# Moving two half products and chunk 4's turns ahead of the work that needs w_out's third quarter

## The chip, the cores and the metric

The kernel runs on one NeuronCore of a Trainium2 chip. The metric is the device time of one execution in microseconds (us). The program has five instruction streams: TensorE (PE in the profile, with its weight loads as PEld), VectorE (DVE), ScalarE (ACT), GpSimd (POOL) and SyncE (SP). Each works through its own stream in the order in which it was written and waits for the others by semaphores. SP issues nearly all transfers; POOL issues the four that bring w_out, because they change the type from float32 to bfloat16 on the way. Sixteen DMA engines carry both.

## The reference

A recurrent attention layer with one decay per head is followed by a feed-forward layer with a squared ReLU. Batch 4, 8 heads, 768 tokens, head size 64; 3072 tokens of width 512; d_ff is 2048.

```
for t in range(S):
    state = gamma[None, :, None, None] * state + einsum('bhd,bhe->bhde', k[:, :, t], v[:, :, t])
    y[:, :, t] = scale * einsum('bhd,bhde->bhe', q[:, :, t], state)
x = y.transpose(0, 2, 1, 3).reshape(B * S, H * D)
h = maximum(x @ w_in, 0.0)
out = h * h @ w_out
```

## The kernel before

**Tiling.** The 3072 tokens are 24 chunks of 128 tokens, six to a batch. The attention is done chunk by chunk: q and k are scaled by powers of the decay and turned (transposed) so that the head dimension lies on the partitions, the scores of a chunk are formed and masked, the running state is updated, and the outputs become the columns of `xt`, the input of the feed-forward part. The feed-forward part works on blocks of chunks: `BLOCKS` makes the first block four chunks wide and the other ten two chunks wide. A block's first product is `x @ w_in` with ReLU (line 826 for the matmuls, 835 for the ReLU on ACT, 806 for the square on DVE); its second product is `h @ w_out`.

**Seven products for eight.** The second product is in part done as a 2 by 2 block product with seven half-width products instead of eight, on sums of blocks. For the weights these sums are the four tiles `w_sum` (t1 to t4), each made in two halves by `sum_w_out` (line 319): the low half of each needs the first two quarters of w_out, the high half the last two. For the first block, chunks 0 and 1 are multiplied in the plain way and chunks 2 and 3 by seven products. That is `second_products` in `last_of_first`. A call `plain(j)` multiplies two of the sixteen row blocks of w_out for chunks 0 and 1 (four matmuls with 512 columns, line 1017) and adds one matmul with 256 columns to the product pa (line 984). `plain(0)` to `plain(3)` use w_out's first two quarters, `plain(4)` and `plain(5)` the third quarter, `plain(6)` and `plain(7)` the fourth. The products pd (s1 by t1), pb (s2 by t2) and pe (a22 by t4) each have eight matmuls with 256 columns; their low halves (four matmuls, `lo`) need only the low halves of t1, t2 and t4.

**What sets the order.** The order is written out by hand. The feed-forward pieces are generators, and each `yield` ends a piece. After piece n the loop at the end calls `before(n)`, which emits whatever `put(n, ...)` has listed for that place. So PE's order is the pieces with the steps of the next chunks' attention between them, and every other engine gets its part of a step at the same point of its own stream. For chunk m, `attend(m, scaled, places)` lists q's turn at `places[0]` (line 391, copied out of PSUM by ACT at line 397), k's turn at `places[1]` (line 404, copied by ACT at line 411), the scores of the first four heads at `places[2]` and of the other four at `places[3]` (line 430, masked by DVE at line 437), the state also at `places[3]` (line 458, copied by ACT at 481 and DVE at 483), and the outputs at `places[4]` (lines 498 and 506, copied by ACT at 514). Both turns use the one PSUM buffer `tp`, so k's turn waits until ACT has copied q's. The two halves of the scores share the one PSUM buffer `st`.

**The places around the change.** Twelve pieces of the first product end at place 16. In `second_products` the pieces `plain(0)` to `plain(5)` end at places 17 to 22; pd's and pb's low halves at 23; pe's low half at 24; `plain(6)` at 25 and `plain(7)` at 26, where ACT copies pa away (line 1038) and the two plain results (line 1041); pa's remaining eight matmuls, which add to the pa just copied, at 27; pd's high half at 28, pb's at 29, pe's at 30. The w_out sums' low halves are listed at place 20; DVE's sums for s3 and s4 (`last_sums`, line 980) at 22.

**Later chunks.** From chunk 8 on, k is scaled and cast on POOL (line 688) and turned by a transposing transfer that SP issues (line 711, tile `kT`), and the scores are at line 727. SP works through loads, stores and these transfers in one order.

Of the kernel before, what the change touches and what calls it, by code (L numbers as in the profile page):

```python
# [31 lines left out]
def kernel(  # L32
# [280 lines left out]
    def sum_w_out(half):  # L313

        src = w_out_halves[half].rearrange("s (j k) (n c) -> s k n j c", k=2, n=2)
        (b11, b12), (b21, b22) = ([src[:, k, n] for n in range(2)] for k in range(2))
        t1, t2, t3, t4 = (t[:, 4 * half : 4 * half + 4] for t in sums)
        for out, in0, in1 in ((t1, b12, b11), (t2, b22, t1), (t3, b22, b12), (t4, b21, t2)):
            yield nc.vector.tensor_tensor(out=out, in0=in0, in1=in1, op=ALU.subtract)
# [498 lines left out]
    def h_of(tb, f0, f1=None):  # L818
        n = NFB // len(h2s[tb])
        j, f = divmod(f0, n)  # L820
        return h2s[tb][j][:, f : f + (1 if f1 is None else f1 - f0)]
# [137 lines left out]
    def last_of_first():  # L959

        def halves_of(k, c):
            return [
                t.rearrange("e (j k) (c t) -> e k c j t", k=2, c=4)[:, k, 2 + c] for t in h2s[0]
            ]

        (a11, a12), (a21, a22) = ([halves_of(k, c) for k in range(2)] for c in range(2))
        n = NFB // 4
        s1, s2, s4 = (
            [
                t.rearrange("e (x j t) -> e x j t", x=2, t=C)[:, x]  # L970
                for x in range(2)
            ]
            for t in (spare[:, i * HN * 4 : (i + 1) * HN * 4] for i in range(3))
        )
        s3 = a21
        b = lambda k, c: lambda j: w_out_bf[j // 2][:, 2 * (j % 2) + k, c * HN : (c + 1) * HN]
        t1, t2, t3, t4 = (lambda j, t=t: t[:, j] for t in sums)

        def add(out, in0, in1, op=ALU.add):
            nc.vector.tensor_tensor(out=out, in0=in0, in1=in1, op=op)  # L980

        def product(to, left, right, js, start=True, stop=True):
            for j in js:
                nc.tensor.matmul(  # L984
                    to,
                    lhsT=left[j // n][:, j % n],
                    rhs=right(j),
                    start=(start and j == 0),
                    stop=(stop and j == NFB // 2 - 1),
                    skip_group_check=True,  # L990
                )

        def first_sums(x):
            add(s1[x], a21[x], a22[x])
            add(s2[x], s1[x], a11[x], ALU.subtract)

        def last_sums():
            for x in range(2):
                add(s3[x], a11[x], a21[x], ALU.subtract)
            for x in range(2):  # L1000
                add(s4[x], a12[x], s2[x], ALU.subtract)

        def second_products():
            ops = [ps_f.tile([P, DM], FP32, name="psf") for _ in range(2)]
            pa, pe, pd, pb = (
                t[:, n * HN : (n + 1) * HN]
                for t in [ps_f.tile([P, DM], FP32, name="psf") for _ in range(2)]
                for n in range(2)
            )
            oa, ob = (opool.tile([P, DM], FP32, name="osb") for _ in range(2))  # L1010
            a, u, v = (upool.tile([P, HN], FP32, name=f"u{i}") for i in range(3))
            r0 = 2 * C

            def plain(j):
                for f in (2 * j, 2 * j + 1):
                    for c, op in enumerate(ops):
                        nc.tensor.matmul(  # L1017
                            op[:],
                            lhsT=h_of(0, f)[:, 0, c * C : (c + 1) * C],
                            rhs=w_out_bf[f // FPQ][:, f % FPQ, :],  # L1020
                            start=(f == 0),
                            stop=(f == NFB - 1),
                        )
                product(pa, a11, b(0, 0), (j,))

            lo, hi = range(0, 4), range(4, 8)
            for j in range(6):
                plain(j)
                yield
            product(pd, s1, t1, lo)  # L1030
            product(pb, s2, t2, lo, False)
            yield
            product(pe, a22, t4, lo, False)
            yield
            plain(6)
            yield
            plain(7)
            nc.scalar.activation(a[:], pa, AF.Copy)
            for c, op in enumerate(ops):
                osb = opool.tile([P, DM], FP32, name="osb")  # L1040
                nc.scalar.activation(osb[:], op[:], AF.Copy)
                nc.sync.dma_start(out[c * C : (c + 1) * C], osb[:])
            yield
            product(pa, a12, b(1, 0), lo, False)
            product(pa, a12, b(1, 0), hi, False)
            nc.scalar.activation(oa[:, 0:HN], pa, AF.Copy)
            yield
            product(pd, s1, t1, hi)
            yield
            product(pb, s2, t2, hi)  # L1050
            add(u[:], pb, a[:])
            yield
            product(pe, a22, t4, hi)
            yield
            product(pb, s3, t3, lo, False)
            yield
            product(pb, s3, t3, hi, False)
            add(v[:], pb, a[:])
            add(ob[:, HN:DM], pd, v[:])
            add(ob[:, 0:HN], pe, v[:])  # L1060

            def last_product():
                product(pd, s4, b(1, 1), range(8), False)
                add(oa[:, HN:DM], pd, u[:])
                yield
                nc.sync.dma_start(out[r0 + C : r0 + 2 * C], ob[:])
                yield
                nc.sync.dma_start(out[r0 : r0 + C], oa[:])
                yield

            kept.append(last_product())
            yield

        return first_sums, last_sums, second_products
# [174 lines left out]
    def put(place, what, *args):  # L1249
        parts.setdefault(place, []).append((what, args))  # L1250
# [4 lines left out]
    def attend(m, scaled, places):  # L1255
        if m % 2 == 0:
            put(scaled, scale_q, m, 0)
            put(scaled + 2 if m == 4 else scaled, scale_q, m, 1)
            put(places[0], transpose_q, m)
        put(18 if m == 4 else places[0], scale_kv, m)  # L1260
        put(places[1], transpose_k, m)
        put(places[2], scores, m, 0)
        put(places[3], scores, m, 1)
        put(places[3], state, m)
        put(places[4], outputs, m)
# [20 lines left out]
    for m, which, place in ((6, "k", 16), (6, "v", 17), (7, "k", 18), (7, "v", 19)):  # L1286
        put(place, load_kv, m, which)
    put(10, cast_w, "in", 3)
    for half, at_places in enumerate(((20, 20, 20, 20), (23, 23, 27, 27))):
        made = sum_w_out(half)  # L1290
        for place in at_places:
            put(place, next, made)
    attend(4, 13, (21, 22, 24, 26, 29))
    attend(5, None, (25, 28, 30, 32, 34))
    attend(6, 31, (33, 35, 37, 39, 42))
    attend(7, None, (38, 42, 44, 46, 49))
# [74 lines left out]
```

## Time and profile before

| what | value |
|---|---|
| median of three runs | 205.26 us (205.23 to 205.27) |
| the profiled execution's own time | 205.27 us |
| its span, first to last instruction | 203.4 us |
| PE busy | 195.3 us (96% of the span) |
| DVE, ACT, POOL busy | 155.2, 127.2, 66.4 us |
| share of the DMA engines' time, SP's queue and POOL's queue | 72.4% and 6.3% |

The span is what the trace covers; 1.87 us of the execution's time lie around it. PE is the engine that is nearly always busy, so time is to be found where PE stands still or where its work can shrink. A gap of another engine costs nothing unless PE waits for what comes behind it. In the views quoted below a row gives the start in us, a length in us, the engine, the line of the kernel, the operation with its tiles, and how many instructions were merged. Brackets give the idle time of the engine before the row and who ended it. A matmul's length includes its drain, which overlaps the next one, so the time that a matmul holds PE is read from start to start.

### The profile page before, as it was taken

To read this page: it belongs to the slowest core of one execution; us is meant where nothing else is said; L and a number is where in the kernel's file an instruction comes from. 1 tells how busy PE (TensorE), PEld (TensorE's weight loads), DVE (VectorE), ACT (ScalarE), POOL (GpSimd) and SP (SyncE) were. 2 spreads that over 40 slices of the span, in tenths; PEclk is the share of its full clock that TensorE was granted. 3 is DMA by queue.
4 is the path that set the end of the run, shared out by engine and by line. 5 is a ranking of instruction groups with operands and counts; after the bars stand their busy time and mean duration, and the time that the engine had idled before them with its cause. 6 is when DMAs were issued, how large, how long until landed. Compare 5 with 4: busy or idle time off the path is not lost.

```text
span 203.4 us, 5804 instructions
## 1 busy us (share of the span) xinstructions
PE 195.3 (96%) x2346; PEld 162.2 (80%) x2351; DVE 155.2 (76%) x322; ACT 127.2 (63%) x258; POOL 66.4 (33%) x131
## 2 busy tenths in 40 slices
PE   5899998999999999999999999999999999999993
PEld 1478444678975998988989899999989999999883
DVE  3986789768797678788698798798798798485374
ACT  8764871455753776792694784783785775763730
POOL 8693710131300451372234335352225225100000
PEclk9999999999999999999999999999999999999999
DMA  5999999999779596989986997899979642200202
GB/s 174 357 374 398 327 190 196 258 232 297 199 197 229 141 158 126 220 216 226 161 228 122 242 215 171 198 228 187 218 168 204 164 103 58 103 3 0 106 0 103
DMA packets 92250, 38.12 MB, mean 187 GB/s; under 512 B 68544, under 2 KB 88256, under 8 KB 92224
## 3 DMA queue, kind: packets, MB, share of 16 engines
q1 hardware_dynamic: 90112, 35.66, 72.4%
q0 software_dynamic: 2112, 2.10, 6.3%
q8 instruction: 18, 0.29, 0.7%
q14 instruction: 8, 0.07, 0.1%
HBM read 27.26 MB, written 6.29 MB: 165 GB/s over the span
## 4 chain that ended last, share of the span: by engine, by line
PE 73%; DMA 11%; SPq 6%; DVE 4%; ACT 3%; issue 1%; POOL 0%; DVEq 0%
PE psf L826 32%; PE psf L860 18%; PE tp L860 7%; DMA w_out_bf<-in_moe_w_out_dram 6%; DMA stage<-in_moe_w_in_dram 5%; PE psf L1149 3%; SPq L164 3%; SPq L115 2%; PE psf L984 2%; PE y L783 2%; PE st L727 2%; PE y L776 2%; PE c_ps L754 2%; PE psf L1017 1%; DVE h L806 1%
## 5 line engine op out<-in xcount | busy, mean ns | idle before, releaser
L826 PE MATMUL psf<-xt,w_in_bf 128*128 128x256 bf16 (+2 forms) x879 | 92.2, 259 | 0.3 <-issue 0.2
L826 PEld LDWEIGHTS <-w_in_bf 128*128 128x128 bf16 x880 | 71.2, 98 | 11.4 <-issue 0.2
L835 ACT ACTIVATE h<-psf 128x512 bf16<-128x512 f32 x96 | 56.1, 595 | 21.7 <-PE psf L826 20.2
L806 DVE TENSOR_TENSOR h<-h 128x512 bf16<-128x512 bf16 x80 | 35.6, 460 | 18.1 <-ACT h L835 17.9
L688 POOL CAST ks_bdp<-stage 64x512 bf16<-64x512 f32 x32 | 23.0, 718 | 37.6 <-issue 23.3
L705 POOL COPY v_bd<-v 64x512 bf16<-64x512 bf16 x32 | 20.6, 644 | 44.8 <-DVE v L697 35.3
L860 PEld LDWEIGHTS <-h 128*128 128x128 bf16 x288 | 26.3, 98 | 3.6 <-DVE h L806 0.7
L860 PE MATMUL tp<-w_out_bf,h 128*128 128x256 bf16 x136 | 19.4, 273 | 0.2 <-DVE h L806 0.2
L860 PE MATMUL psf<-w_sum,h 128*128 128x256 bf16 x136 | 19.1, 273 | 0.0
L860 PE MATMUL psf<-w_sum,k_bd 128*128 128x256 bf16 x144 | 17.9, 273 | 0.0
L361 DVE TENSOR_TENSOR qs<-qn,qf 128x512 bf16<-128x512 f32 x20 | 16.0, 804 | 0.1
L860 PEld LDWEIGHTS <-k_bd 128*128 128x128 bf16 x144 | 13.7, 98 | 1.5
L856 DVE TENSOR_TENSOR osb<-psf,u 128x256 f32<-128x256 f32 x26 | 10.3, 421 | 6.1 <-PE psf L860 5.8
L763 ACT ACTIVATE s_bd<-c_ps 64x256 bf16<-64x256 f32 x29 | 10.7, 370 | 6.3 <-PE c_ps L754 6.3
L856 DVE TENSOR_TENSOR u<-psf,u 128x256 f32<-128x256 f32 x18 | 7.6, 423 | 8.9 <-PE psf L860 8.8
L697 DVE TENSOR_TENSOR v<-stage,kf 128x512 bf16<-128x512 f32 x16 | 12.5, 780 | 0.0
L764 ACT ACTIVATE s_bd<-c_ps 64x256 bf16<-64x256 f32 x29 | 11.0, 379 | 0.4
L734 DVE TENSOR_TENSOR pt<-st,cmask 128x512 bf16<-128x512 f32 x16 | 11.0, 687 | 0.3 <-issue 0.2
L856 DVE TENSOR_TENSOR k_bd<-h 128x512 bf16<-128x512 bf16 x18 | 10.7, 596 | 0.3
L790 ACT ACTIVATE xt<-y 128x512 bf16<-128x512 f32 x16 | 9.6, 598 | 1.8 <-PE y L783 1.2
L896 ACT ACTIVATE osb<-tp 128x256 f32<-128x256 f32 x8 | 3.1, 384 | 12.2 <-PE tp L860 12.2
L804 ACT ACTIVATE h<-h 128x512 bf16<-128x512 bf16 x16 | 10.1, 630 | 0.5
(145 smaller groups left out, 281.6 us busy)
## 6 DMA issues: line engine op xcount, KB each, us to landing
qn<-in_q_dram SPq DMA_DIRECT2D x12, 512.0 KB, 5.1
out_dram<-osb SPq DMA_DIRECT2D x23, 256.0 KB, 3.0
stage<-in_k_dram SPq DMA_DIRECT2D x32, 96.0 KB, 3.8
stage<-in_v_dram SPq DMA_DIRECT2D x32, 96.0 KB, 3.2
stage<-in_moe_w_in_dram SPq DMA_DIRECT2D x4, 512.0 KB, 7.1
stage<-in_moe_w_in_dram SPq DMA_DIRECT2D x2, 1024.0 KB, 10.2
w_out_bf<-in_moe_w_out_dram POOLq DMA_DIRECT2D x4, 512.0 KB, 10.4
kn<-in_k_dram SPq DMA_DIRECT2D x6, 256.0 KB, 5.9
```

What stands on the lines that cost most here:

```text
L361: engine.tensor_tensor(out=out, in0=by, in1=table[:, :, None].to_broadcast([P, H, D]), op=ALU.mult)
L688: nc.gpsimd.tensor_copy(ks[rows, :, hh, :].rearrange("s (u p) d -> s u p d", u=2), kn[rows])
L697: nc.vector.tensor_tensor(out=v2.rearrange("s (u p) d -> s u p d", u=2), in0=vn, in1=kf2[:, i, :, :, None].to_broadcast([P, 2, NPAIR, D]), ...
L705: nc.gpsimd.tensor_copy(v_bd[rows, :, hh, :], v2[rows])
L734: nc.vector.tensor_tensor(out=pt[:], in0=st[:], in1=cmask2.rearrange("s r t -> s (r t)")[:, None, :].to_broadcast([P, 2 * NPAIR, C // 2]), ...
L763: nc.scalar.activation(s_bd[halves[0], :, 0, :], c[halves[0]], AF.Copy)
L764: nc.scalar.activation(s_bd[halves[1], :, 1, :], c[halves[1]], AF.Copy)
L806: nc.vector.tensor_mul(hv, hv, hv)
L826: nc.tensor.matmul(hp, lhsT=w_in_bf[g][:, cb, fq * 128 : (fq + 1) * 128], rhs=xts[tb][:, cb, cols], start=(cb == 0), stop=(cb == NCB - 1),)
L835: nc.scalar.activation(hv, hp[:], AF.Relu)
L856: nc.vector.tensor_tensor(out=out, in0=in0, in1=in1, op=op)
L860: nc.tensor.matmul(to, lhsT=left[:, j], rhs=right(j) if callable(right) else right[:, j], start=(start and j == 0), stop=(stop and j == NF ...
```

## The change

Three orders change; no instruction is added or taken away. In `second_products` the low halves of pd and pb go ahead of `plain(4)` and `plain(5)`, the first pieces that use w_out's third quarter. The places then end at 20 for `plain(3)`, 21 for the two low halves, 22 and 23 for `plain(4)` and `plain(5)`; from 24 on they are as before. Chunk 4's q is turned at 19 instead of 21, its k at 21 instead of 22, its scores and masks come at 23 and 25 instead of 24 and 26, its state at 25 instead of 26; its outputs stay at 29. The high halves of t1 and t2 go from place 23 to 24, those of t3 and t4 from 27 to 26. On DVE this puts chunk 4's first mask ahead of the high halves of t1 and t2, and its second mask and state copy ahead of chunk 5's k scaling.

```diff
@@ -1024,12 +1024,15 @@
                 product(pa, a11, b(0, 0), (j,))
 
             lo, hi = range(0, 4), range(4, 8)
-            for j in range(6):
+            for j in range(4):
                 plain(j)
                 yield
             product(pd, s1, t1, lo)
             product(pb, s2, t2, lo, False)
             yield
+            for j in range(4, 6):
+                plain(j)
+                yield
             product(pe, a22, t4, lo, False)
             yield
             plain(6)
@@ -1286,11 +1289,11 @@
     for m, which, place in ((6, "k", 16), (6, "v", 17), (7, "k", 18), (7, "v", 19)):
         put(place, load_kv, m, which)
     put(10, cast_w, "in", 3)
-    for half, at_places in enumerate(((20, 20, 20, 20), (23, 23, 27, 27))):
+    for half, at_places in enumerate(((20, 20, 20, 20), (24, 24, 26, 26))):
         made = sum_w_out(half)
         for place in at_places:
             put(place, next, made)
-    attend(4, 13, (21, 22, 24, 26, 29))
+    attend(4, 13, (19, 21, 23, 25, 29))
     attend(5, None, (25, 28, 30, 32, 34))
     attend(6, 31, (33, 35, 37, 39, 42))
     attend(7, None, (38, 42, 44, 46, 49))
```

## The prediction

> **What bounds the kernel now.** I read the page first (busy shares and the chain that ended last), then PE's waits between 24 and 60 us, then the order of instructions around them.
>
> ```profile
> PE 195.3 (96%) x2346; PEld 162.2 (80%) x2351; DVE 155.2 (76%) x322; ACT 127.2 (63%) x258; POOL 66.4 (33%) x131
> PEclk9999999999999999999999999999999999999999
> PE 73%; DMA 11%; SPq 6%; DVE 4%; ACT 3%; issue 1%; POOL 0%; DVEq 0%
> PE psf L1017 <- DMA w_out_bf<-in_moe_w_out_dram: 0.9, 1, 0.9
> PE psf L984 <- DVE w_sum L319: 0.2, 1, 0.2
> ```
>
> PE is the bound, at full granted clock. What can be won by reordering is only the time in which PE stands still, and the two waits say where: in the first block's second product, once for w_out's third quarter, once for a sum of w_out. The order of instructions shows more small gaps beside these two.
>
> ```profile
> 33.84 1.03 PE L1017 MATMUL psf<-w_out_bf,h 128*128 128x512 bf16 x4
> 35.86 1.02 PE L1017 MATMUL psf<-w_out_bf,h 128*128 128x512 bf16 x4 [0.88 <-DMA w_out_bf<-in_moe_w_out_dram]
> 36.83 0.61 PE L391 MATMUL tp<-ident,qs 128*128 128x128 bf16 x8
> 37.27 1.03 PE L1017 MATMUL psf<-w_out_bf,h 128*128 128x512 bf16 x4
> 37.47 1.02 ACT L397 ACTIVATE qT<-tp 128x1024 bf16<-128x1024 bf16 x1 [5.75 <-PE tp L391]
> 38.55 0.38 PE L404 MATMUL tp<-ident,ks 128*128 128x128 bf16 x4
> 38.77 1.47 PE L984 MATMUL psf<-w_sum,h 128*128 128x256 bf16 x12
> 38.97 1.21 ACT L411 ACTIVATE k_bd<-tp 64x512 bf16<-64x512 bf16 x2 [0.47 <-PE tp L404]
> 39.27 0.69 DVE L319 TENSOR_TENSOR w_sum<-w_out_bf 128x1024 bf16<-128x1024 bf16 x1 [1.29 <-DMA w_out_bf<-in_moe_w_out_dram]
> 40.08 0.49 PE L430 MATMUL st<-qT,k_bd 128*128 128x128 bf16 x4
> 40.41 1.03 PE L1017 MATMUL psf<-w_out_bf,h 128*128 128x512 bf16 x3
> 41.38 1.03 PE L1017 MATMUL psf<-w_out_bf,h 128*128 128x512 bf16 x4
> 42.35 0.39 PE L430 MATMUL st<-qT,k_bd 128*128 128x128 bf16 x4
> 42.55 0.38 ACT L1038 ACTIVATE u<-psf 128x256 f32<-128x256 f32 x1 [2.38 <-PE psf L984]
> 42.58 0.39 PE L458 MATMUL c_ps<-v_bd,ks 128*128 128x128 bf16 x4
> 42.78 0.69 DVE L437 TENSOR_TENSOR pt<-st,cmask 128x512 bf16<-128x512 f32 x1 [0.88 <-PE st L430]
> 42.99 1.03 PE L984 MATMUL psf<-w_out_bf,h 128*128 128x256 bf16 x8
> 44.96 0.22 PE L498 MATMUL y<-qT,s_bd 128*128 128x128 bf16 x1
> 45.25 0.68 DVE L319 TENSOR_TENSOR w_sum<-w_out_bf,w_sum 128x1024 bf16<-128x1024 bf16 x1
> 45.99 0.61 PE L984 MATMUL psf<-w_sum,h 128*128 128x256 bf16 x4 [0.20 <-DVE w_sum L319]
> 47.83 1.06 PE L826 MATMUL psf<-xt,w_in_bf 128*128 128x128 bf16 x16
> ```
>
> Start to start, a `plain` piece holds PE 0.97 us (35.86 to 36.83, 40.41 to 41.38), eight turns 0.44 (36.83 to 37.27), four turns, four scores or four state matmuls 0.22 to 0.23 (38.55 to 38.77, 42.35 to 42.58), and twelve half-width matmuls 1.31 (38.77 to 40.08), so 0.109 each: four take 0.44, eight 0.87. Chunk 4's outputs are twelve matmuls of 128 columns, 0.67 at the turns' pace. With these the gaps come out: before `plain(4)` 33.84 + 0.97 = 34.81 to 35.86, **1.05**; before k's turn 37.27 + 0.97 = 38.24 to 38.55, **0.31** (one `tp`: ACT frees it at 38.49); in the first scores 0.33 less 0.23, **0.10** (ACT's copy of k ends at 40.18); before pa's remaining matmuls 42.58 + 0.22 = 42.80 to 42.99, **0.19** (ACT must copy pa first); before pe's high half 44.96 + 0.67 = 45.63 to 45.99, **0.36** (the high half of t4 on DVE ends at 45.93).
>
> **The change part by part.** PE does the same work; I walk it from 33.84, where chunk 4's q turn now stands.
>
> ```profile
> 31.13 0.60 ACT L835 ACTIVATE h<-psf 128x512 bf16<-128x512 f32 x1 [0.27 <-PE psf L826]
> 30.37 0.68 DVE L361 TENSOR_TENSOR qs<-qn,qf 128x512 bf16<-128x512 f32 x1
> 34.34 0.69 DVE L319 TENSOR_TENSOR w_sum<-w_out_bf,w_sum 128x1024 bf16<-128x1024 bf16 x1
> 35.55 1.10 DVE L319 TENSOR_TENSOR w_sum<-w_out_bf,w_sum 128x1024 bf16<-128x1024 bf16 x1
> 37.24 0.74 DVE L980 TENSOR_TENSOR h<-h,h 128x512 bf16<-128x512 bf16 x2
> 44.20 0.43 DVE L483 CAST s_bd<-c_ps 64x256 bf16<-64x256 f32 x1 [0.73 <-ACT s_bd L481]
> ```
>
> *q's turn and `plain(3)`.* q was scaled by 31.05 (30.37 + 0.68), and ACT has nothing between 31.73 and 37.47. Turn 33.84 to 34.28, `plain(3)` to 35.25. ACT copies 0.64 after the turn's start (36.83 to 37.47): 34.48 to 35.50. *The two half products ahead* need the low halves of t1 and t2, ready at 35.03 (34.34 + 0.69): 35.25 to 36.12, no wait. *k's turn* finds `tp` free since 35.50: to 36.34, so the 0.31 goes; ACT copies k 0.42 later (38.55 to 38.97), 36.54 to 37.75. *`plain(4)`* starts at 36.34 where the quarter was usable at 35.86: the 1.05 goes, with 0.48 to spare. `plain(5)` ends at 38.28. *First scores:* k's copy has been done for half a microsecond, so the 0.10 goes; to 38.50. pe's low half (t4 done at 36.65) to 38.94.
>
> *What is late next, the fourth quarter.* DVE could use it at 39.27, after standing idle for it. Before, PE came to `plain(6)` at 40.41 and this arrival was hidden; now it comes at 38.94. I take 39.27 for PE too: a new wait of **0.33**. `plain(6)` to 40.24, scores and state to 40.68.
>
> *`plain(7)` and pa.* From `plain(7)`'s start to pa's remaining matmuls before was 42.99 - 41.38 = 1.61, of which 0.97 is the piece; the rest is ACT's copy (42.55 to 42.93) with the handovers. Before, scores and state lay in it and PE lost 0.19; now they have gone ahead, nothing covers it, and PE waits 0.64, **0.45** more. ACT's state copy goes ahead of the pa copy, but its state is done 0.97 earlier. pa starts at 40.68 + 1.61 = 42.29.
>
> *t4 in time.* DVE now does, in order: first mask (0.43 after the scores' start, as 42.35 to 42.78: 38.71 to 39.40, behind the sums of line 980 that end at 37.98), high t1, high t2, second mask, state copy, chunk 5's k scaling, high t3, high t4. Six of about 0.69 and one 0.43 with no overlap end at 39.40 + 4.57 = 43.97. Should one run 1.10, as the row at 35.55 did, it is 44.38. pe's high half comes at 42.29 + 0.87 + 0.44 + 0.22 + 0.44 + 0.67 = 44.93: the 0.36 goes with half a microsecond to spare at the worst. Queued behind the new wait on DVE are the second mask and chunk 5's scaling, wanted only by its k turn at 43.60. That turn's copy on ACT (0.42 later, 44.02 to 45.23) must be done by the scores at 45.37: 0.14 to spare, which is tight.
>
> *SP and POOL* keep their order; before 44 us no transfer on them waits for what is moved, so I leave the landings where they are.
>
> From pa's remaining matmuls to the next block's first product the old way took 47.83 - 42.99 = 4.84, less 0.36 is 4.48: **42.29 + 4.48 = 46.77, a gain of 1.06 us.** By the gaps: 1.05 + 0.31 + 0.10 + 0.36 - 0.33 - 0.45 = 1.04, the same but for rounding. The profiled execution took 205.27 us (median of the runs 205.26), so 204.2. If the new waits cost nothing the gain would be 1.82, but the 0.45 is a turnaround that the trace shows in full; only the 0.33 is open, from zero (204.2 - 0.33 = 203.9) to the late landing below.
>
> The Trainium skill, "TensorE: Matmul & The Clock Gate", section "Back-to-back issue gap", gives about 131 ns per 512-column and 81 ns per 128-column matmul in a sustained stream. By it, as an estimate with this kernel's rows for the half-width ones, PE would stand before `plain(6)` at 38.33 instead of 38.94, the fourth quarter would cost 0.61 more, and the time would be 204.8. The trace disagrees: a piece of four 512-column matmuls and one of 256 takes 0.97, of which the four are 0.86, or 215 ns each.
>
> **The rivals.**
>
> ```profile
> L170 POOL DMA_DIRECT2D w_out_bf<-in_moe_w_out_dram x4: 742/767/940, 21.9 to 25.3; - x4
> ...
> DMA to landing us min/median/max: 7.1/10.4/13.9
> ...
> kn<-in_k_dram SPq DMA_DIRECT2D x1, 256.0 KB, 15.7
> 78.37 1.27 SPq L711 DMA_TRANSPOSE kT<-ks_bdp  x1
> kT<-ks_bdp SPq DMA_TRANSPOSE x1, 3.3
> kT<-ks_bdp SPq DMA_TRANSPOSE x1, 4.2
> 82.32 0.40 PE L727 MATMUL st<-qT,kT 128*128 128x64 bf16 x8
> ```
>
> *A: transfers that don't move take some back.* PE is 1.06 us early for every later load. The nearest later case is chunk 10's turned k: issued by SP at 78.37, landed 3.3 later at 81.67, used at 82.32. If SP's order doesn't come earlier with PE, PE arrives at 81.26 and waits 0.41: 204.6. For it: SP is busy without a break through these stretches. Against it: part of SP's order waits for stores that PE and ACT release.
>
> *B: no gain is left.* The same transfer at the 4.2 us that chunk 11's took would land at 82.57, later than PE came before: 205.3 or a little over. It needs SP unmoved and a slower landing, both; I give it little.
>
> *C, the slower end: w_out's fourth quarter lands late.* The longest landing of the four w_out transfers, 13.9 us, is this quarter's, from its issue at 25.3 to 39.2. Behind it now stand PE's `plain(6)` and DVE's second mask with nothing to cover them, so each microsecond counts in full. The gain is gone when it lands 1.06 later, at 40.3; at the 15.7 us that chunk 5's k load took in the same stretch it lands at 41.0, 1.73 later than the 39.27: 204.2 + 1.7 = 205.9. Against it: what SP and POOL issue before that is unchanged. The Trainium skill, "DMA: Bandwidth & Descriptors", section "Queues, rings and completion order", says that each DMA engine takes turns between its queues packet by packet; by that, more packets on SP's queue would delay w_out. No row here shows those turns one by one.
>
> **How the numbers follow.** The walk as told 0.67, with 203.9 to 204.4 as its own range; the fourth quarter costing nothing 0.05 (203.9); A 0.13 (204.6); B 0.07; C 0.08. The forecast is the walk's 204.2. The range, 203.8 to 204.9, takes the first three cases, 0.85. About 0.2% (0.4 us) is what can be told from no change: faster 0.85, same 0.07, slower 0.08.
>
> **What would show it.** In the changed profile the wait for w_out's third quarter is gone from PE's list and a wait of about 0.3 us for the fourth stands in front of `plain(6)`; the turn of k follows the half products without a gap; a gap of some 0.6 us stands between `plain(7)` and the next half-width matmuls; no wait for `w_sum` is left; the next block's first product starts near 46.8; chunk 10's scores start near 81.3 without a wait. The prediction is wrong if either quarter's landing moves by more than half a microsecond, or if the gain at 46.8 is not there at the end.

## The result and the profile after

| | before | changed |
|---|---|---|
| median of 18 executions each | 205.29 us (205.16 to 206.04) | 204.52 us (204.05 to 205.28) |
| mean of the same | 205.50 us | 204.59 us |
| ratio of the times | | 0.9956, 95% interval 0.9943 to 0.9968 |
| the profiled execution's own time, span | 205.27, 203.4 us | 204.98, 203.1 us |

The changed kernel is faster by 0.44%: 0.9 us by the ratio and by the means, 0.77 by the medians, 1.11 between the quickest executions. The forecast was 204.2. Both kernels' times here can be split at their widest gap into two groups: 204.05 to 204.57 (eleven) and 204.79 to 205.28 (seven) for the changed one, 205.16 to 205.30 (ten) and 205.53 to 206.04 (eight) for the one before.

The page of the changed kernel, engine shares and chain, and PE's waits between 24 and 60 us:

```profile
PE 195.3 (96%) x2351; PEld 162.2 (80%) x2351; DVE 154.7 (76%) x322; ACT 127.5 (63%) x258; POOL 67.5 (33%) x131
PE 88%; DVE 4%; DMA 3%; ACT 2%; SPq 1%; issue 1%; DVEq 0%
PE psf L984 <- ACT u L1041: 0.5, 1, 0.5
```

PE is as busy as before. The two waits of this stretch, for w_out's third quarter and for a sum of w_out, are gone; a wait of pa's remaining matmuls for ACT is new (the changed file's line 1041 is the pa copy, 1038 before). The chain has 3% of transfers where it had 11%.

PE's order in the changed kernel, from chunk 4's q turn to the next block's first product (rows left out are marked by dots):

```profile
34.61 0.61 PE L391 MATMUL tp<-ident,qs 128*128 128x128 bf16 x8
...
39.92 1.02 PE L1017 MATMUL psf<-w_out_bf,h 128*128 128x512 bf16 x4
...
45.58 0.60 PE L984 MATMUL psf<-w_sum,h 128*128 128x256 bf16 x4
46.02 0.39 PE L430 MATMUL st<-qT,k_bd 128*128 128x128 bf16 x4
...
47.41 0.78 PE L826 MATMUL psf<-xt,w_in_bf 128*128 128x128 bf16 x11
```

From q's turn the stretch takes 47.41 - 34.61 = 12.80 us; before, from the same PE time, it took 47.83 - 33.84 = 13.99. That is 1.19 won. But q's turn itself stands 0.77 later in this execution (34.61 against 33.84), so the next block's product is only 0.42 earlier, and 0.14 is lost further on: 0.28, the difference of the two spans to rounding. The 0.77 doesn't come from the diff. Most of it arose in the program's first 10 us, ahead of everything that the diff moves, as the first scaling on GpSimd shows (changed kernel, then the kernel before):

```profile
8.25 1.23 POOL L559 TENSOR_TENSOR ks_bdp<-kn,kfp 128x512 bf16<-128x512 f32 x1 [2.12 <-DMA kn<-in_k_dram]
```

```profile
7.60 1.26 POOL L559 TENSOR_TENSOR ks_bdp<-kn,kfp 128x512 bf16<-128x512 f32 x1 [1.46 <-DMA kn<-in_k_dram]
```

The first k arrived 0.65 later here; in the later run of the changed kernel (experiment 12) this scaling started at 7.71. So two questions were left for the experiments: are the steps right where the start is the same as in the profile of before, and what does a late start do to either kernel?

### The profile page after: what moved, and what is told of

Its sections match the earlier page's. It is cut to its first block, busy times and chain, and to the rows that moved or that the text cites. A ratio compares the mean times of both kernels' runs of the same rounds, so it can differ in the third digit from the quotient of the medians.

```text
span 203.1 us, 5810 instructions
## 1 busy us (share of the span) xinstructions
PE 195.3 (96%) x2351; PEld 162.2 (80%) x2351; DVE 154.7 (76%) x322; ACT 127.5 (63%) x258; POOL 67.5 (33%) x131
## 4 chain that ended last, share of the span: by engine, by line
PE 88%; DVE 4%; DMA 3%; ACT 2%; SPq 1%; issue 1%; DVEq 0%
PE psf L826 40%; PE psf L860 18%; PE tp L860 7%; PE psf L1017 3%; PE psf L1152 3%; DMA kn<-in_k_dram 3%; PE psf L984 3%; PE y L783 2%; PE st L727 2%; PE y L776 2%; PE c_ps L754 2%; DVE h L806 1%; PE c_ps L627 1%; PE y L506 1%; PE st L430 1%
## 5 line engine op out<-in xcount | busy, mean ns | idle before, releaser
L896 ACT ACTIVATE osb<-tp 128x256 f32<-128x256 f32 x8 | 3.1, 384 | 12.2 <-PE tp L860 12.2
```

## The experiments

**1 and 2: each part alone.** The first keeps the half products' move and puts chunk 4's places and the sums back; the second keeps the places and leaves the products where they were.

```diff
 e1: the changed kernel with
-    for half, at_places in enumerate(((20, 20, 20, 20), (24, 24, 26, 26))):
+    for half, at_places in enumerate(((20, 20, 20, 20), (23, 23, 27, 27))):
-    attend(4, 13, (19, 21, 23, 25, 29))
+    attend(4, 13, (21, 22, 24, 26, 29))
 e2: the changed kernel with
-            for j in range(4):
+            for j in range(6):
                 plain(j)
                 yield
             product(pd, s1, t1, lo)
             product(pb, s2, t2, lo, False)
             yield
-            for j in range(4, 6):
-                plain(j)
-                yield
```

> The half products of pd and pb go ahead of plain(4) and plain(5); chunk 4's places and the w_out sums stay as before. Theory (the gain is PE's wait for the third quarter, everything else only moves from one gap to another): the 1.05 us in front of plain(4) goes, the gaps at k's turn (0.31), at t4 (0.36) and at pa (0.19) stay, no wait for the fourth quarter appears since PE comes to it at about 40.3; the stretch from plain(3)'s start to the next block's first product, 13.99 us before, shrinks by 1.1, as much as in the whole change (predicted 1.06, 1.19 in its profile). Rival (the places carry a good part): it shrinks by 0.7 or less. Time 204.2 against 205.27 by the theory, 204.6 or more by the rival.

> Chunk 4's places and the places of the w_out sums as in the change; the half products stay behind plain(5). Theory: q's turn now stands in front of plain(3), so 0.44 us of the wait for the third quarter is covered and 0.61 is left; the gaps at k's turn (0.31), first scores (0.10) and t4 (0.36) go; pa's wait grows from 0.19 to 0.64; no wait for the fourth quarter, which PE reaches at 39.6. The stretch shrinks by 0.77: time 204.5. Rival (the places only move waits about): the stretch shrinks by 0.4 or less, what q's turn covers.

Measured: the products alone 204.28 us (204.10 to 205.37), ratio 0.9964 (0.9948 to 0.998); the places alone 204.90 us (204.46 to 205.06), ratio 0.9975 (0.9967 to 0.9984). PE's order with the products alone:

```profile
30.92 0.81 PE L1017 MATMUL psf<-w_out_bf,h 128*128 128x512 bf16 x3
...
36.13 1.03 PE L1017 MATMUL psf<-w_out_bf,h 128*128 128x512 bf16 x4
...
37.41 0.38 PE L404 MATMUL tp<-ident,ks 128*128 128x128 bf16 x4
...
44.85 0.61 PE L984 MATMUL psf<-w_sum,h 128*128 128x256 bf16 x4 [0.20 <-DVE w_sum L319]
...
46.69 0.50 PE L826 MATMUL psf<-xt,w_in_bf 128*128 128x128 bf16 x6
```

The third quarter's wait is gone (`plain(4)` at 36.13, right behind the turn of q); the waits for `tp` (0.31 before 37.41) and for t4 stay, and pa is not late (41.85, 0.11 behind the state). The block's product starts at 46.69, 1.14 earlier than before. So in this execution the products alone bring as much as the whole change (46.65, below): the places save the small gaps and pay for them with the pa wait and the fourth quarter. The places alone, in an execution whose `plain(0)` was late:

```profile
31.95 0.81 PE L1017 MATMUL psf<-w_out_bf,h 128*128 128x512 bf16 x3
...
36.29 1.03 PE L1017 MATMUL psf<-w_out_bf,h 128*128 128x512 bf16 x4
...
43.02 1.03 PE L984 MATMUL psf<-w_out_bf,h 128*128 128x256 bf16 x8 [0.47 <-ACT u L1038]
...
47.48 0.72 PE L826 MATMUL psf<-xt,w_in_bf 128*128 128x128 bf16 x10
```

PE came to the third quarter (`plain(4)`, 36.29) 1.03 later than it would have from an early start and found it landed: where the start is late there is no such wait to take away. So the wait of 0.61 that was expected to be left could not be seen here. The three quickest executions, 204.46 to 204.61, are where the expected 204.5 lies, but none of them was profiled. The start is thus a term of its own.

**3 to 6: a late PE, and a late fourth quarter, in both kernels.** Five matmuls of 512 columns whose result nobody reads (1.08 us of PE) are added at place 14, ahead of the first block's second product; or two copies on GpSimd into an unused tile (1.57 us) between the third and the fourth w_out transfer.

```diff
 e5 (before) and e6 (changed)
     put(10, cast_w, "in", 3)
+    put(14, keep_awake, 5, 4 * C, ps_y, "y")
+    put(14, end_awake)
 e7 (before) and e8 (changed)
+    idle_sb = spare[:, 3072:3584].rearrange("s (j t) -> s j t", t=P)
     for g, place in enumerate((6, 8, 11, 14)):
+        if g == 3:
+            for _ in range(2):
+                put(place, nc.gpsimd.tensor_copy, idle_sb, ident[:, None, :].to_broadcast([P, 4, P]))
         put(place, load_w_out, g)
```

> The kernel before with five matmuls of 512 columns that nobody uses (5 x 0.215 = 1.08 us of PE work) added at place 14, ahead of the second product. Theory: before, PE stood 1.05 us for w_out's third quarter, so PE that comes later by that much loses nothing there; the time rises by 0.0 to 0.1 (205.3), and the wait in front of plain(4) is gone from the trace. Rival (what is added to PE is added to the time): +1.08, 206.3.

> The changed kernel with the same five matmuls at place 14. Theory: the change has taken out the wait that hid a late PE; only the 0.33 us in front of plain(6) can hide any of the 1.08, so the time rises by 0.75 over the changed kernel's own (204.1 in its quickest runs): 204.85, and the gap between the two kernels shrinks from 1.1 to about 0.4. Rival (a late PE is hidden in both): 204.1 to 204.2.

> The kernel before with two copies on POOL (128 by 512, about 0.65 us each, to a tile part that nobody reads) between the issues of w_out's third and fourth quarter, so that the fourth is issued some 1.3 us later. Theory: PE comes to plain(6) at 40.4 and the quarter then lands at 39.3 plus at most 1.3, so at most 0.2 us are lost: 205.3 to 205.5. The third quarter may land a little earlier, which would win up to 0.2.

> The changed kernel with the same delay. Theory: nothing covers the fourth quarter any more, so each microsecond by which it lands later counts in full: if its landing moves by 1.3, the wait in front of plain(6) grows from 0.2 or 0.3 to 1.5 and the time rises by 1.3, to 205.4 in the quickest runs, as slow as the kernel before. Rival (DMA engines are full in this stretch, so a later issue does not move the landing): no change, 204.1 to 204.5.

*The late PE.* The kernel before with it: 205.68 us (205.29 to 206.34), ratio 1.0016 (0.9998 to 1.0034). The changed kernel with it: 205.51 us (204.98 to 206.63), ratio 1.0 (0.9977 to 1.0024). Quickest against quickest, the 1.08 us cost the kernel before 0.13 to 0.17 (205.29 against 205.16 and 205.12) and the changed one 0.93 (204.98 against 204.05, which is from the runs of the result). The order in the kernel before with the late PE:

```profile
32.01 1.03 PE L1017 MATMUL psf<-w_out_bf,h 128*128 128x512 bf16 x4
...
35.95 1.02 PE L1017 MATMUL psf<-w_out_bf,h 128*128 128x512 bf16 x4
...
47.92 1.06 PE L826 MATMUL psf<-xt,w_in_bf 128*128 128x128 bf16 x16
```

`plain(0)` starts 1.08 later than before, `plain(4)` only 0.09, the next block 0.09. The wait for the third quarter swallowed it. It was not only a loss but also slack, and the change spends it. The changed kernel with the five matmuls was profiled in its slowest execution (206.63), which started late besides:

```profile
33.03 1.03 PE L1017 MATMUL psf<-w_out_bf,h 128*128 128x512 bf16 x4
...
48.56 0.61 PE L826 MATMUL psf<-xt,w_in_bf 128*128 128x128 bf16 x8
```

`plain(0)` is 2.11 later than from an early start (30.92), the next block 1.91 later than the 46.65 that is shown below: what PE loses ahead of this place now reaches the next block, less the 0.2 of the fourth quarter's wait.

*The late fourth quarter.* Before: 205.73 us (205.31 to 206.53), ratio 1.0015 (0.9997 to 1.0033); in its profile the next block stood at 47.73, 0.10 earlier than without the copies, and five of its ten executions took 206.05 or more, which was not expected. Changed: 204.95 us (204.27 to 205.13), ratio 0.9969 (0.9954 to 0.9984). The issue and landing times of the four w_out transfers in the changed kernel with the copies:

```profile
L170 POOL DMA_DIRECT2D w_out_bf<-in_moe_w_out_dram x4: 742/764/940, 21.9 to 26.9; - x4
...
DMA to landing us min/median/max: 7.1/10.3/12.2
```

The fourth was issued 1.6 us later than in the profile of before and took 12.2 us where it had taken 13.9: it landed at 39.1 against 39.2. My theory that this later issue moves the landing fell, and the condition of the slower rival (a landing after 40.3) could not be made this way, so what such a landing would cost was not tested. The run served for something else: its first loads came as early as in the profile of before and the landing had not moved, so it shows the change from the same start.

```profile
30.92 1.03 PE L1017 MATMUL psf<-w_out_bf,h 128*128 128x512 bf16 x4
...
36.13 0.39 PE L404 MATMUL tp<-ident,ks 128*128 128x128 bf16 x4
36.36 1.03 PE L1017 MATMUL psf<-w_out_bf,h 128*128 128x512 bf16 x4
...
38.52 0.60 PE L984 MATMUL psf<-w_sum,h 128*128 128x256 bf16 x4
39.17 1.02 PE L1017 MATMUL psf<-w_out_bf,h 128*128 128x512 bf16 x4
...
40.58 1.03 PE L1017 MATMUL psf<-w_out_bf,h 128*128 128x512 bf16 x4
...
42.19 1.03 PE L984 MATMUL psf<-w_out_bf,h 128*128 128x256 bf16 x8 [0.47 <-ACT u L1041]
...
44.83 0.60 PE L984 MATMUL psf<-w_sum,h 128*128 128x256 bf16 x4
...
46.65 0.55 PE L826 MATMUL psf<-xt,w_in_bf 128*128 128x128 bf16 x7
...
81.14 0.40 PE L727 MATMUL st<-qT,kT 128*128 128x64 bf16 x8
```

The next block starts at 46.65, 1.18 earlier than before; chunk 10's scores at 81.14, also 1.18 earlier; this execution has a span of 202.2, 1.2 less. All that was won in the first block is there at the end of the span; its time, 204.27, is only 1.00 less, as 0.2 more lies outside the span.

**7 to 10: the two gaps that the change leaves.** One edit puts pd's high half between `plain(7)` and pa's remaining matmuls, to stand over ACT's copy of pa. The other lists chunk 4's scores one place later and the high halves of t3 and t4 one earlier. Both are run alone, then together; the first a second time.

```diff
 e3, e10: the changed kernel with
+            product(pd, s1, t1, hi)
             product(pa, a12, b(1, 0), lo, False)
             product(pa, a12, b(1, 0), hi, False)
             nc.scalar.activation(oa[:, 0:HN], pa, AF.Copy)
             yield
-            product(pd, s1, t1, hi)
             yield
 e4: the changed kernel with
-    for half, at_places in enumerate(((20, 20, 20, 20), (24, 24, 26, 26))):
+    for half, at_places in enumerate(((20, 20, 20, 20), (24, 24, 25, 25))):
-    attend(4, 13, (19, 21, 23, 25, 29))
+    attend(4, 13, (19, 21, 24, 26, 29))
 e9: both
```

> The change, with pd's high half (four matmuls, 0.44 us) moved from behind pa's remaining matmuls to in front of them. Theory (pa's 0.6 us wait is a plain turnaround through ACT that independent PE work covers): the gap behind plain(7) shrinks from 0.64 to about 0.2 and the stretch is 0.44 shorter than the change's: 203.8. Rival (ACT becomes the limit: k's copy of chunk 5 stands behind three copies of results and the scores of chunk 5 wait for it): most of the 0.44 comes back in front of the scores of chunk 5, 204.1 to 204.2.

> The change, but chunk 4's scores, masks and state stay at their old places 24 and 26, with all four high halves of the w_out sums at 24 and 25. Theory: scores and state lie again between plain(7) and pa and cover 0.45 us of its turnaround, so the gap there is 0.2 and the stretch 0.44 shorter than the change's: 203.8. The wait for the fourth quarter stays at 0.33. Rival (the masks are needed early: the second mask now ends at 43.7, just before chunk 4's outputs at 43.8): PE waits in front of the outputs and the gain is 0.2 or less, 204.0 or more.

> Chunk 4's scores back at places 24 and 26 with the w_out sums' high halves at 24 and 25, and pd's high half ahead of pa's remaining matmuls: scores, state and pd's half, 0.89 us, now lie between plain(7) and pa's remaining matmuls, whose turnaround takes 0.64. Theory (gaps add up): the gap of 0.2 that either alone leaves there is gone too, the quickest runs come at 203.4 to 203.5, 0.2 below either alone. Rival (chunk 4's masks or chunk 5's k copy on ACT become late for PE): no better than 203.65, the quickest of either alone.

> The change with pd's high half first, once more on the same chip as the version with the scores back, so that the two can be compared: quickest runs at 203.65 as before, by the theory 0.2 above the combined version.

| edit | median, us | range, us | ratio, 95% interval | next block in the profiled execution |
|---|---|---|---|---|
| pd first | 203.85 | 203.64 to 204.53 | 0.9933 (0.9920 to 0.9946) | 46.23 |
| scores back | 203.81 | 203.67 to 204.88 | 0.9937 (0.9919 to 0.9955) | 47.05, late start |
| both | 204.30 | 203.78 to 205.14 | 0.9946 (0.9925 to 0.9967) | 46.85, late start |
| pd first again | 204.07 | 203.56 to 205.66 | 0.9940 (0.9921 to 0.9958) | 46.16 |

PE's order around pa with pd first:

```profile
41.56 0.60 PE L984 MATMUL psf<-w_sum,h 128*128 128x256 bf16 x4
42.20 1.03 PE L984 MATMUL psf<-w_out_bf,h 128*128 128x256 bf16 x8
...
46.23 0.94 PE L826 MATMUL psf<-xt,w_in_bf 128*128 128x128 bf16 x14
```

The four matmuls (0.44) fill the wait down to 0.20, and the block starts 0.42 earlier than with the change alone (46.65): the wait of 0.64 in front of pa was a real cost on the path. Each edit alone is about 0.2% under the changed kernel, by intervals that overlap its own a little. With the scores back the gap in front of pa's remaining matmuls was 0.19 as expected. Whether both together beat one is not settled: the quickest, 203.78, missed the expected 203.4 to 203.5, and the ratios overlap throughout. In the traces of the scores edit and of both edits, each with a late start, the gap was gone with both and the next block stood 0.20 earlier (46.85 against 47.05), which is what the gaps add up to. One execution of the pd edit took 205.66 us, the longest of its kind, and its trace shows why:

```profile
112.97 0.41 PE L727 MATMUL st<-qT,kT 128*128 128x64 bf16 x8 [1.89 <-DMA kT<-ks_bdp]
...
109.44 1.27 SPq L711 DMA_TRANSPOSE kT<-ks_bdp  x1
```

SP issued that turned k, chunk 14's, at 109.44; in the first run of the same code the corresponding issue stood at 106.16. What made the issue late was not followed further.

**11 and 12: where the late start comes from.** In the profiled executions whose `plain(0)` stood near 31.95 instead of 30.92 (with the five added matmuls, 33.03 instead of 32.01), PE had waited 0.9 to 1.2 us, some 10 us into the program, for a scaling of chunk 2's k on VectorE (line 559), whose second half GpSimd scales at the same time. One edit gives both halves to VectorE; beside it the changed kernel runs once more.

```diff
-    scale_pair_k(2, 1, nc.gpsimd)
+    scale_pair_k(2, 1)
```

> The changed kernel with chunk 2's second half of the scaled k (scale_pair_k(2, 1)) on VectorE instead of GpSimd. Theory: the spread of the changed kernel's times comes from VectorE and GpSimd meeting at that line (VectorE's scaling 0.69 us or 1.24 to 1.34 us, GpSimd's 1.04 or 1.55 us, the projections' first product at 30.92 or 31.95 us in the runs so far). With one engine alone no scaling of that line takes over 1 us on VectorE, the price is one more VectorE instruction of 0.69 us in the front (by at most that, 204.05 + 0.2 to 0.6 for the quickest), and the times lie closer together: median 204.3 to 204.8, spread under 0.7 us against 1.2 us of the changed kernel. Rival: the spread comes from when the first loads land (6.1 or 6.7 us): it stays 1 us or more, and the median is that of the changed kernel plus the price, 204.7 to 205.2.

> The changed kernel once more, beside the one with the scaling on VectorE alone. Both theories: median 204.4 to 204.8, from 204.0 to 205.3, ratio to the kernel before 0.995 to 0.997; with the chunk's scaling the only difference between the two kernels, a narrower spread in the other is due to it.

Measured: all on VectorE 204.17 us (204.01 to 204.44), ratio 0.9942 (0.9929 to 0.9955); the changed kernel 204.62 us, ratio 0.9964 (0.995 to 0.9977). Its eight times form two groups, four from 204.12 to 204.34 and four from 204.89 to 205.08; the five with the edit form one, close to the lower. The scalings of line 559 in the kernel before, whose start was early, and in the changed kernel of this run, whose start was late:

```profile
8.98 0.69 DVE L559 TENSOR_TENSOR ks_bdp<-kn,kfp 128x512 bf16<-128x512 f32 x1
...
9.03 1.55 POOL L559 TENSOR_TENSOR ks_bdp<-kn,kfp 128x512 bf16<-128x512 f32 x1 [0.17 <-DMA kn<-in_k_dram]
```

```profile
9.21 1.50 DVE L559 TENSOR_TENSOR ks_bdp<-kn,kfp 128x512 bf16<-128x512 f32 x1
...
9.12 1.04 POOL L559 TENSOR_TENSOR ks_bdp<-kn,kfp 128x512 bf16<-128x512 f32 x1 [0.18 <-DMA kn<-in_k_dram]
...
PE c_ps L584 <- DVE ks_bdp L559: 1.2, 1, 1.2
...
31.95 1.03 PE L1017 MATMUL psf<-w_out_bf,h 128*128 128x512 bf16 x4
...
47.48 1.06 PE L826 MATMUL psf<-xt,w_in_bf 128*128 128x128 bf16 x16
```

Whoever starts second waits. Where VectorE starts first, at 8.98, it takes 0.69 and GpSimd's takes 1.55; where GpSimd is first, by 0.09, its takes 1.04 and VectorE's 1.50, and ends at 10.71 instead of 9.67. Those 1.04 us are the 1.03 by which `plain(0)` is late. The other traces sort the same way: in five GpSimd's scaling led, by 0.09 to 0.52 us, and VectorE's took 1.07 to 1.50; in the seven in which VectorE's led it took 0.69. With both halves on VectorE:

```profile
9.30 0.68 DVE L559 TENSOR_TENSOR ks_bdp<-kn,kfp 128x512 bf16<-128x512 f32 x1
...
10.50 0.68 DVE L559 TENSOR_TENSOR ks_bdp<-kn,kfp 128x512 bf16<-128x512 f32 x1
...
31.43 1.03 PE L1017 MATMUL psf<-w_out_bf,h 128*128 128x512 bf16 x4
```

Neither scaling on VectorE takes over 0.7 us, and the start is 0.5 late instead of 1.03. Five executions are few; that the upper group is gone with the edit speaks for the theory, against the rival that the first loads alone make the spread. So does the first scaling on GpSimd: outside the profile of the changed kernel it began at 7.60 to 7.71, in early and late starts alike. That the loads make part of the spread, the profile of the changed kernel shows: there the scalings took 0.69 and 1.55 and the start was late with the loads.

The meeting of the two scalings has a cause of its own, further up. VectorE's scaling stands behind its first mask, which waits for PE's first scores: the mask began at 8.26 in the kernel before and at 8.60 in the changed kernel of the last run. PE was late with them: the same four turns, at 6 us, took it longer (kernel before, then the changed kernel of the last run):

```profile
6.00 0.40 PE L550 MATMUL st<-ident,qs 128*128 128x128 bf16 x4
```

```profile
6.05 0.61 PE L550 MATMUL st<-ident,qs 128*128 128x128 bf16 x4
```

They took 0.40 to 0.49 in the seven traces in which VectorE led, and 0.61 in the five in which GpSimd did and in the one with both halves on VectorE; one more trace, with 0.61 here but the short length from 6.9 on, had the two scalings start 0.01 apart. So the moment at which PE comes to its full pace sorts the starts, and the meeting of the two engines makes 1.03 us at `plain(0)` out of the 0.34 that it costs the mask. The granted clock in the profile's rows is 1.00 on both sides, and why that moment moves was not tested. All of it stands ahead of what the diff moves, and the kernel before begins with the same instructions.

## Why the prediction was right

*The steps, from the same start.* k's turn stood at 36.13 (predicted 36.12), `plain(4)` at 36.36 (36.34), without a wait. PE came to the fourth quarter at 38.52 + 0.44 = 38.96 (38.94) and waited 0.21 where I had 0.33: the quarter that DVE took up at 39.27 before was usable to PE at 39.17. From `plain(7)` to pa's remaining matmuls 42.19 - 40.58 = 1.61, the predicted turnaround exactly, with its wait of 0.64. pe's high half needed no wait at 44.83 (44.93). The next block came at 46.65 (46.77). The only term that was off is the fourth quarter's, by 0.12. The copies on GpSimd didn't make that: with pd first and no copies `plain(6)` stood at 39.18 from the same start. The Trainium skill's rule of a shorter spacing for 512-column matmuls ("TensorE: Matmul & The Clock Gate", "Back-to-back issue gap") is not borne out here: the piece still takes 0.97 (36.36 to 37.33), and the 0.61 that it would have added did not come.

*t4 and chunk 5.* In the same-start profile t4 was done at 43.76 (predicted 43.97). In the profile of the changed kernel, whose PE is 0.77 later, DVE's last sum and ACT's copy of chunk 5's k are these:

```profile
43.82 0.72 DVE L319 TENSOR_TENSOR w_sum<-w_out_bf,w_sum 128x1024 bf16<-128x1024 bf16 x1
```

```profile
44.67 1.21 ACT L411 ACTIVATE k_bd<-tp 64x512 bf16<-64x512 bf16 x2 [0.28 <-PE tp L404]
```

t4 is done at 44.54, a microsecond ahead of pe's high half at 45.58. The copy ends at 45.88 for scores at 46.02: the predicted 0.14 to spare.

*The rivals.* A and B needed chunk 10's turned k to stay where it was. SP issued it earlier than PE moved, at 75.61 where it had been 78.37, and PE did not wait:

```profile
75.61 1.38 SPq L711 DMA_TRANSPOSE kT<-ks_bdp  x1
```

So A and B fell for this chunk. But it was not the nearest case, as the prediction has it. Chunk 14's turned k was nearer in the kernel before:

```profile
109.01 1.28 SPq L711 DMA_TRANSPOSE kT<-ks_bdp  x1
...
112.57 0.40 PE L727 MATMUL st<-qT,kT 128*128 128x64 bf16 x8
```

It took 3.5 us to land, so about 0.06 was to spare, where chunk 10's had 0.65. By A's own sum an issue that didn't come earlier would have taken nearly all of the gain there. In the changed kernel SP issued it at 107.24, and at 106.12 in the same-start profile, and PE did not wait; in the pd edit's execution with an issue at 109.44 it waited 1.89. So A happens, in some executions.

C's landing after 40.3 was not seen, but the fourth quarter did move. In the profile of the changed kernel, with its late first loads, it was issued 0.9 later than before and landed at 39.9, 0.7 later:

```profile
L170 POOL DMA_DIRECT2D w_out_bf<-in_moe_w_out_dram x4: 740/766/937, 22.8 to 26.2; - x4
...
DMA to landing us min/median/max: 7.0/10.2/13.7
```

That is more than the half microsecond which the prediction had named as a sign of being wrong. PE was 0.77 later as well, and waited only 0.18. With early loads it landed at 39.1 to 39.3 in the seven profiles with an early start, the copies on GpSimd among them, and at 39.3 to 39.9 in the five with a late one.

*What the sum lacked.* The forecast of 204.2 is right for an execution that starts like the profiled one (quickest 204.05; 204.27 with the copies on GpSimd), but the median is 204.52 and the mean gain 0.91, not 1.06. The median lies above the walk's own range (203.9 to 204.4) and near A's 204.6, so it is the traces, not the time, that tell the walk from A. One account of the difference is the late start. The walk took the old wait of 1.05 as pure loss. A PE that came 1.08 late cost the kernel before only 0.09 in the first block, while the changed kernel pays for it: with the late start of the last run its next block stood at 47.48, against 46.65 with the early one. A late PE at nearly the same place put the kernel before at 47.92. So the change brings 47.83 - 46.65 = 1.18 from an early start and about 47.92 - 47.48 = 0.44 from a late one. If the upper four of the last run's eight executions are its late starts (one of them was profiled), that would be 0.8 on average, near the measured 0.77 and 0.9. The 0.44 compares two different causes of a late PE (`plain(0)` at 32.01 and at 31.95); the kernel before was not profiled with the meeting of the two scalings itself.

The times speak against this account. By it a late start costs the kernel before about 0.1, so its times should form one group, but eight of the eighteen are about 0.6 above the others on average. Group by group the change wins 0.90 in the lower (205.24 and 204.34 on average) and 0.85 in the upper (205.83 and 204.98), so the gain may be about the same from either start. No execution of the upper group of the kernel before was profiled. It may be its late starts, or waits such as chunk 14's, with its 0.06 to spare; that stays open, and with it what share of the shortfall the start has.

*What each part does.* From a late start the places alone reach the same 47.48 as the whole change, from an early one the products alone nearly the same 46.69 as its 46.65. The products thus help when PE is early at the third quarter, the places when it is late. The slowest times agree: the four late ones of the products alone lie at 205.25 to 205.37, those of the whole change in the last run at 204.89 to 205.08. No trace of those four was taken, nor of the whole change without the late start and without another edit, so that reading is argued, not shown.

## What to carry to other kernels

A wait on the critical path for a transfer is also slack: before you forecast what removing it brings, ask how much the work ahead of it varies from one execution to the next, and count only the part of the wait that is there each time. Here 1.08 us of added work in front of the wait moved the next block by 0.09. When steps are moved out of a gap, look at what they were covering: ACT's copy of pa cost 0.64 us once the scores and state had gone ahead, and four other matmuls in their place won back 0.42.

## What the runs showed of the hardware

- VectorE and GpSimd, each multiplying two SBUF tiles, do not share the time; the one that starts first keeps its pace. A lead of 0.04 or 0.05 us for VectorE gave 0.69 and 1.55 us, GpSimd's ending 0.90 or 0.91 after VectorE's; a lead of 0.09 to 0.52 us for GpSimd gave 1.04 for it and 1.07 to 1.50 for VectorE, ending 0.54 or 0.55 after GpSimd's. At the next block that is 0.83 us here, and the two groups of the last run's times are 0.67 apart. The Trainium skill, "SBUF — State Buffer", section "Who interferes with whom", states that a VectorE instruction with two SBUF inputs contends with a GpSimd instruction that reads SBUF, and that the order of issue decides which of the two is blocked. The rows agree.
- A w_out transfer issued 1.6 us later landed at the same time (13.9 us from issue to landing became 12.2), but where the first loads were 0.65 late too it was issued 0.9 later and landed 0.7 later. The page shows the DMA engines 90% busy or more in the slices of this stretch; I take it that they, and not the issue, set the landing; no run here separates that from other causes.
- PE's same four turns at about 6 us took 0.40 us in some executions and 0.61 in others, with a granted clock of 1.00 in the rows of both; the starts of the second product sort by it.
